# Feature projections in float32 on half the array, two items at a time, in a linear-attention and expert-MLP kernel

## The chip, the cores and the metric

The kernel runs on one core of a Trainium2 chip. The metric is the time of one execution on the device in microseconds (us). The engines are called as in the profile: PE (TensorE, with its weight loads as PEld), DVE (VectorE), ACT (ScalarE), POOL (GpSimd) and SP (SyncE, which issues most DMAs).

## The reference

Three layers in a row: linear attention with exponential features, a gated MLP, and a mixture of four experts. Only the first is touched by the change.

```python
batch, n_heads, seq, head_dim, d_feat = 2, 8, 576, 64, 128
def phi(x):
    proj = np.einsum('bhsd,df->bhsf', x, w_phi)
    proj = proj - np.max(np.abs(proj), axis=-1, keepdims=True)
    return np.concatenate([np.exp(proj), np.exp(-proj)], axis=-1)
q_p, k_p = phi(q), phi(k)
kv = np.einsum('bhsf,bhsd->bhfd', k_p, v)
z = np.sum(k_p, axis=2)
num = np.einsum('bhsf,bhfd->bhsd', q_p, kv)
den = np.einsum('bhsf,bhf->bhs', q_p, z)[..., None] + 1e-06
x = num / den                       # to [1152, 512]
x = ((x @ w_a) * (x @ w_b)) @ w_out # 1152 x 512, inner size 1536
out = sum over e of p[:, e] * (relu(x @ w1[e]) @ w2[e])   # 4 experts, inner size 1024
```

All inputs are float32.

## The kernel before

Heads are worked on in pairs: the 64 dimensions of one head lie on partitions 0 to 63, those of its partner on 64 to 127. A tile is 128 positions of a head pair. Since 576 is four tiles and a half, the half tiles of two head pairs share one tile, marked "m". An **item** is two tiles; there are 18 items for k and then 18 for q, nine for each of the two batches. Three items make a chunk of 768 columns of the transposed k or q, which SP loads as `xraw` (`load_chunk`).

One loop over slots writes the program of the attention (lines 765 to 803), and this hand-written order is the order of each engine's queue. Slot s issues, in this sequence:

- `split_x(s + 3)`: ACT rounds 256 columns of `xraw` to float32r (`xp`, high part) and POOL subtracts to get the low part, three slots ahead.
- `stage_proj(s)`: six float32r matmuls of 128 rows and 256 columns into one PSUM tile `pj`. The right side `wbp` is block diagonal: w_phi for head 0 in rows 0 to 63 and columns 0 to 127, for head 1 in the rest, zeros elsewhere. Three matmuls (high by high, high by low, low by high) make one tile. Then DVE takes the largest magnitude (`mx`) and subtracts it (`r`); for k, ACT makes the two exponentials (`kp`).
- `stage_kv(s - 3)` for k items: four float32 matmuls of 128 rows and 256 columns, or for an "m" tile four of 64 rows, which add to `kv`. A finished head pair is copied from PSUM by DVE (`kvt`), transposed on PE two slots later (`kz`) and copied again (`kvz`, by DVE in the first batch and by ACT in the second).
- `stage_rt(s - 4)` for q items: four PE transposes of `r` (`rt`), then ACT's exponentials (`qp`).
- What fell due: `stage_num` (eight float32 matmuls of 288 columns, `num`, read by ACT into `den` and `x`), one slot later `stage_x` on DVE (transpose of `den` to `dt`, reciprocal `rc`, spread back over `dt`, transpose to `rb`, product with `x`), then `stage_xparts` (`xh` on ACT, `xl` on POOL).
- Preparation of the weights of the MLP (`prep`: `begin` on ACT, `middle` on DVE, `parts` on ACT and POOL) in every second k slot and in the last slots, and in the last slots the first matmuls of the MLP (`unit_ab`).

The PSUM tiles of `pj`, `kz`, `rt` and `ab` share the pool `u` with four buffers; `kv` and `num` share `nd` with two. Behind the attention come `unit_ab`, `o1`, `unit_h` and `o2`, which make the two MLPs.

Of the kernel before, what the change touches and what calls it, by code (L numbers as in the profile page):

```python
# [9 lines left out]
F32 = mybir.dt.float32  # L10
F32R = mybir.dt.float32r
# [36 lines left out]
def tile_linear_attention_then_mlps(ctx, tc, qT, kT, v, w_phi, wab, wout, w12, probs, out):  # L48
# [19 lines left out]
    m_p = None  # L68
    l_p = None

    wb = r_p.tile([128, 2, 128], F32, tag="wb", name="wb")
    wbp = r_p.tile([128, 2, 256], F32R, tag="wbp", name="wbp")

    with tc.manual_schedule():
        nc.scalar.dma_start(out=wb[0:64, 0, :], in_=w_phi)
        nc.scalar.dma_start(out=wb[64:128, 1, :], in_=w_phi)
        nc.vector.memset(wb[0:64, 1, :], 0.0)
        nc.vector.memset(wb[64:128, 0, :], 0.0)

        nc.vector.memset(psm, 0.0)  # L80
        nc.scalar.activation(out=psm, in_=psm, func=AF.Exp)
# [1 line left out]
        def two_parts(hi, lo, src, eng):  # L83
            nc.scalar.activation(out=hi, in_=src, func=AF.Copy)  # L84
            eng.tensor_tensor(out=lo, in0=src, in1=hi.bitcast(F32), op=ALU.subtract)  # L85

        NC = 3 * 256
        xraw = {}
        xpart = {}

        def load_chunk(n):


            if n >= 2 * B * 3:
                return
            t = r_p.tile([128, NC], F32, tag="xraw", name="xraw", bufs=2)
            src = (kT if n < B * 3 else qT)[n % (B * 3)]
            step = 256 if n == 0 else NC
            for c in range(0, NC, step):
                nc.sync.dma_start(out=t[:, c:c + step], in_=src[:, c:c + step])  # L100
            xraw[n] = t

        def split_x(i, eng):
            n, c = i // 3, i % 3 * 256
            if c == 0:
                xpart[n] = [r_p.tile([128, NC], F32R, tag=f"xp{k}", name="xp", bufs=2) for k in range(2)]
            hi, lo = (t[:, c:c + 256] for t in xpart[n])
            if i == 0:
                nc.vector.tensor_copy(hi, xraw[n][:, 0:256])
                nc.vector.tensor_tensor(out=lo, in0=xraw[n][:, 0:256], in1=hi.bitcast(F32), op=ALU.subtract)  # L110
            else:
                two_parts(hi, lo, xraw[n][:, c:c + 256], eng)
            if c == 512:
                load_chunk(n + 2)
# [32 lines left out]
        for kind in "kq":  # L147
            for b in range(B):
                for g in range(9):
                    items.append((kind, b, g, seq[2 * g:2 * g + 2]))  # L150

        st_r = {}
        st_kp = {}
        kv_ps = {}
        kvt_t = {}
        kvz_t = {}
        qp_t = {}

        def stage_proj(i):
            kind, b, g, ts_ = items[i]  # L160
            ps = u_p.tile([128, 2, 2, 128], F32, tag="u", name="pj")
            for j in range(2):
                c = i % 3 * 256 + j * 128
                hi, lo = (t[:, c:c + 128] for t in xpart[i // 3])
                o = ps[:, j].rearrange("p h f -> p (h f)")
                nc.tensor.matmul(out=o, lhsT=hi, rhs=wbp[:, 0], start=True, stop=False)
                nc.tensor.matmul(out=o, lhsT=hi, rhs=wbp[:, 1], start=False, stop=False)
                nc.tensor.matmul(out=o, lhsT=lo, rhs=wbp[:, 0], start=False, stop=True)
            ps4 = ps.rearrange("p t h f -> p (t h) f")
            mx = r_p.tile([128, 4], F32, tag="mx", name="mx", bufs=4)  # L170
            nc.vector.tensor_reduce(out=mx, in_=ps4, op=ALU.max, axis=AX.X, apply_absolute_value=True)
            r = r_p.tile([128, 4, 128], F32, tag="r", name="r", bufs=6)
            nc.vector.tensor_tensor(
                out=r, in0=ps4, in1=mx.unsqueeze(2).to_broadcast([128, 4, 128]), op=ALU.subtract
            )
            st_r[i] = r
            if kind == "k":
                kp = k_p.tile([128, 4, 2, 128], F32, tag="kp", name="kp", bufs=4)
                nc.scalar.activation(out=kp[:, :, 0, :], in_=r, func=AF.Exp)
                nc.scalar.activation(out=kp[:, :, 1, :], in_=r, func=AF.Exp, scale=-1.0)  # L180
                st_kp[i] = kp

        def stage_kv(i):
            kind, b, g, ts_ = items[i]
            kp = st_kp[i]
            done = []
            for j, t in enumerate(ts_):
                if t[0] == "m":
                    parts = [(t[1], 4, 0, 64, False, True), (t[2], 4, 64, 128, True, False)]
                else:  # L190
                    first, last = t[1] == 0, t[1] == 3
                    parts = [(t[0], t[1], 0, 128, first and t[0] % 2 == 0, last and t[0] % 2 == 1)]
                for p, st, lo, hi, first, last in parts:
                    if first:
                        kv_ps[b, p] = nd_p.tile([128, 2, 512], F32, tag="nd", name="kv")
                    for h in range(2):
                        nc.tensor.matmul(
                            out=kv_ps[b, p][:, h, 0:256],
                            lhsT=vt[b][lo:hi, st, p, 64 * h:64 * h + 128],
                            rhs=kp[lo:hi, 2 * j + h].rearrange("p s f -> p (s f)"),  # L200
                            start=first, stop=last,
                        )
                    if last:
                        done.append((b, p))
            for b, p in done:
                t = k_p.tile([128, 2, 256], F32, tag="kvt", name="kvt", bufs=2)
                nc.vector.tensor_copy(t, kv_ps.pop((b, p))[:, :, 0:256])
                kvt_t[b, p] = t
            return done

# [2 lines left out]
        def stage_kvz(b, p):  # L213
            src = kvt_t.pop((b, p))
            ps = u_p.tile([128, 2, 2, 128], F32, tag="u", name="kz")
            for h in range(2):
                for s in range(2):
                    nc.tensor.transpose(out=ps[:, h, s, :], in_=src[:, h, 128 * s:128 * s + 128], identity=ident)
            t = kvz_all[:, b * NP + p].rearrange("p (h s f) -> p h s f", h=2, s=2)
            if b == B - 1:  # L220
                nc.scalar.activation(out=t, in_=ps, func=AF.Copy)
            else:
                nc.vector.tensor_copy(t, ps)
            kvz_t[b, p] = t

        def stage_rt(i):
            kind, b, g, ts_ = items[i]
            r = st_r[i]
            ps = u_p.tile([128, 2, 2, 128], F32, tag="u", name="rt")
            for j in range(2):  # L230
                for h in range(2):
                    nc.tensor.transpose(out=ps[:, h, j, :], in_=r[:, 2 * j + h, :], identity=ident)
# [55 lines left out]
            return x, den  # L288

        def stage_x(b, p, x, den):  # L290
            dt = q_p.tile([128, 18, 32], F32, tag="dt", name="dt", bufs=1)
            nc.vector.transpose(out=dt.rearrange("p a b -> p (a b)"), in_=den.rearrange("p a b -> p (a b)"))
            rc = q_p.tile([128, 18, 1], F32, tag="rc", name="rc", bufs=2)
            nc.vector.reciprocal(out=rc, in_=dt[:, :, 0:1])
            nc.vector.tensor_copy(dt, rc.to_broadcast([128, 18, 32]))
            rb = q_p.tile([128, 2, HT], F32, tag="rb", name="rb", bufs=1)
            nc.vector.transpose(out=rb.rearrange("p a b -> p (a b)"), in_=dt.rearrange("p a b -> p (a b)"))
            nc.vector.tensor_tensor(out=x, in0=x, in1=rb, op=ALU.mult)
# [408 lines left out]
        def run(gen, rate, tasks_per):  # L707
# [13 lines left out]


        load_chunk(0)
        load_chunk(1)
        alloc_v(0)
        load_v(0, 0)
        load_v(0, 1)
        make_identity(nc, ident)
        split_x(0, nc.vector)
        nc.vector.tensor_copy(wbp[:, 0], wb.rearrange("p h f -> p (h f)"))  # L730
        nc.vector.tensor_tensor(
            out=wbp[:, 1], in0=wb.rearrange("p h f -> p (h f)"), in1=wbp[:, 0].bitcast(F32), op=ALU.subtract
        )
        for i in range(1, 3):
            split_x(i, nc.vector)
        for st in range(2, 5):
            load_v(0, st)
        alloc_v(1)

        def probabilities():  # L740
# [24 lines left out]
        for slot in range(NI + 9):  # L765
            if slot < NI:
                kind, b, g, ts_ = items[slot]
                if slot + 3 < NI:
                    split_x(slot + 3, nc.gpsimd)
                stage_proj(slot)  # L770
            if slot == NK + 4:
                for fn, a in todo.pop(slot, []):
                    fn(*a)
# [109 lines left out]
```

## Time and profile before

| | us |
|---|---|
| median of 3 runs (lowest to highest) | 731.62 (731.14 to 731.96) |
| the profiled execution | 731.71 |
| its span, first to last instruction | 729.8 |
| PE busy | 716.4 (98%) |
| DVE busy | 431.0 (59%) |
| ACT busy | 325.8 (45%) |
| POOL busy | 304.0 (42%) |

The busy times hold for the whole span. The attention is the first seventh of it, and there the shares are others than on average, so the stages are to be read one by one. The profile models the end of a matmul; the distance of two starts tells more than the length of a row. An entry in brackets at a row's end is the idle time of the engine before it and what ended it.

### The profile page before, as it was taken

Reading aid. Unit: us, or ns where it says so; the run is one execution under the profiler, and the core shown is the slowest. Engines: PE = TensorE matmul, PEld = TensorE weight load, DVE = VectorE, ACT = ScalarE, POOL = GpSimd, SP = SyncE. Lnnn points to the kernel's source line nnn. Section 1 sums busy time; section 2 is a strip of 40 time slices with the busy share of each in tenths; the row PEclk is TensorE's granted clock in tenths of the full one; section 3 lists DMA queues with packets and bytes.
Section 4 is the critical chain, followed back from the end, with each engine's and each line's share of the span. In section 5 each row is a group of like instructions: output and inputs, shape, how many; then the busy total and the mean of one; then the engine's idle time right before and its main releaser. Section 6 shows DMA issues by size and latency. Waiting matters only on the chain.

```text
span 729.8 us, 11577 instructions
## 1 busy us (share of the span) xinstructions
PE 716.4 (98%) x4544; PEld 660.2 (90%) x4544; DVE 431.0 (59%) x737; ACT 325.8 (45%) x658; POOL 304.0 (42%) x277
## 2 busy tenths in 40 slices
PE   7999999999999999999899999999999999999998
PEld 6887879999999999999789898988988898989896
DVE  5997987566666664363635454545455545545454
ACT  5787996655444442233644232323233333423221
POOL 3664435554444343312783434434352535343300
PEclk9999999999999999999999999999999999999999
DMA  8643001332323231012031112110111111100003
GB/s 232 190 131 116 1 30 30 116 96 79 115 64 106 64 87 30 11 49 87 3 114 30 43 46 58 30 58 30 58 55 33 31 58 58 30 30 0 1 1 129
DMA packets 37798, 46.18 MB, mean 63 GB/s; under 512 B 5616, under 2 KB 26608, under 8 KB 37744
## 3 DMA queue, kind: packets, MB, share of 16 engines
q1 hardware_dynamic: 37440, 45.25, 20.7%
q8 instruction: 35, 0.57, 0.3%
q10 hardware_dynamic: 304, 0.20, 0.1%
q14 instruction: 19, 0.16, 0.1%
HBM read 43.08 MB, written 2.36 MB: 62 GB/s over the span
## 4 chain that ended last, share of the span: by engine, by line
PE 85%; DVE 8%; ACT 3%; DMA 2%; issue 1%; POOL 0%; DVEq 0%; SPq 0%; POOLq 0%
PE acc L680 9%; PE acc L679 9%; PE acc L678 9%; PE ab L608 6%; PE ab L606 6%; PE ab L607 6%; PE X L531 5%; PE X L532 5%; PE X L533 5%; PE acc L637 3%; PE acc L638 3%; PE acc L636 3%; PE num L275 3%; PE Z L532 2%; PE Z L531 2%; PE Z L533 2%
## 5 line engine op out<-in xcount | busy, mean ns | idle before, releaser
L694 DVE SCALAR_TENSOR_TENSOR oacc<-acc,pr,oacc 128x512 f32<-128x512 f32 (+1 forms) x136 | 101.3, 746 | 117.5 <-PE acc L680 117.5
L85 POOL TENSOR_TENSOR w<-wx,w 128x512 fp32r<-128x512 f32 x68 | 91.5, 1346 | 155.2 <-ACT w L84 155.2
L85 POOL TENSOR_TENSOR wc<-wt,wc 128x512 fp32r<-128x512 f32 (+1 forms) x48 | 70.0, 1490 | 109.6 <-ACT wc L84 109.6
L680 PE MATMUL acc<-w,hhb 128*128 128x512 f32 x288 | 114.0, 396 | 0.9 <-DVE hhb L655 0.9
L606 PE MATMUL ab<-xh,w 128*128 128x288 f32 x384 | 113.5, 296 | 0.0
L608 PE MATMUL ab<-xh,w 128*128 128x288 f32 x384 | 113.1, 295 | 0.0
L679 PE MATMUL acc<-w,hhb 128*128 128x512 f32 x288 | 113.1, 393 | 0.0
L607 PE MATMUL ab<-xl,w 128*128 128x288 f32 x384 | 113.0, 294 | 0.0
L678 PE MATMUL acc<-w,hhb 128*128 128x512 f32 x288 | 112.7, 391 | 0.0
L654 ACT ACTIVATE hhb<-h 128x288 fp32r<-128x288 f32 x64 | 36.2, 565 | 96.2 <-DVE h L539 96.1
L531 PE MATMUL X<-xc,wc 128*128 128x288 f32 x256 | 77.2, 301 | 1.4 <-ACT h L536 1.4
L532 PE MATMUL X<-xc,wc 128*128 128x288 f32 x256 | 75.8, 296 | 0.7 <-DVE xc L85 0.7
L533 PE MATMUL X<-xc,wc 128*128 128x288 f32 x256 | 75.4, 295 | 0.0
L536 ACT ACTIVATE h<-X 128x288 f32<-128x288 f32 x64 | 26.0, 407 | 104.7 <-PE X L533 104.7
L607 PEld LDWEIGHTS ab<-xl,w 128*128 128x128 f32 x384 | 72.0, 188 | 0.1
L606 PEld LDWEIGHTS ab<-xh,w 128*128 128x128 f32 x384 | 72.0, 188 | 0.1
L608 PEld LDWEIGHTS ab<-xh,w 128*128 128x128 f32 x384 | 72.0, 188 | 0.0
L680 PEld LDWEIGHTS acc<-w,hhb 128*128 128x128 f32 x288 | 54.0, 188 | 15.7 <-DVE hhb L655 4.4
L376 POOL TENSOR_TENSOR wx<-wx,rn 128x512 uint32<-128x512 uint32 x36 | 47.0, 1306 | 50.8 <-DVE wx L373 50.8
L655 DVE SCALAR_TENSOR_TENSOR hhb<-h,hhb 128x288 fp32r<-128x288 f32 x64 | 40.5, 633 | 42.2 <-ACT hhb L654 42.2
L679 PEld LDWEIGHTS acc<-w,hhb 128*128 128x128 f32 x288 | 54.0, 188 | 8.4
L678 PEld LDWEIGHTS acc<-w,hhb 128*128 128x128 f32 x288 | 54.1, 188 | 7.7
(104 smaller groups left out, 1655.0 us busy)
## 6 DMA issues: line engine op xcount, KB each, us to landing
raw<-in_wab SPq DMA_DIRECT2D x24, 512.0 KB, 3.8
wt<-in_w SPq DMA_DIRECT2D x64, 128.0 KB, 2.4
wx<-in_w SPq DMA_DIRECT2D x32, 256.0 KB, 3.0
raw<-in_wout SPq DMA_DIRECT2D x12, 512.0 KB, 3.7
xraw<-in_qT SPq DMA_DIRECT2D x6, 384.0 KB, 3.1
out<-oacc SPq DMA_DIRECT2D x8, 256.0 KB, 2.0
xraw<-in_kT SPq DMA_DIRECT2D x5, 384.0 KB, 3.6
v<-in_v SPq DMA_DIRECT2D x8, 192.0 KB, 4.4
```

The source lines that it names most:

```text
L85: eng.tensor_tensor(out=lo, in0=src, in1=hi.bitcast(F32), op=ALU.subtract)
L376: nc.gpsimd.tensor_tensor(out=x, in0=x, in1=r, op=ALU.add)
L531: nc.tensor.matmul(out=ps, lhsT=whi, rhs=xhi, start=first and a == 0, stop=False, skip_group_check=True)
L532: nc.tensor.matmul(out=ps, lhsT=whi, rhs=xlo, start=False, stop=False, skip_group_check=True)
L533: nc.tensor.matmul(out=ps, lhsT=wlo, rhs=xhi, start=False, stop=a == 1, skip_group_check=True)
L606: nc.tensor.matmul(out=t, lhsT=whi, rhs=hi, start=(c == 0), stop=False)
L607: nc.tensor.matmul(out=t, lhsT=whi, rhs=lo, start=False, stop=False)
L608: nc.tensor.matmul(out=t, lhsT=wlo, rhs=hi, start=False, stop=(c == KD - 1))
L678: nc.tensor.matmul(out=acc, lhsT=hi, rhs=w[:, 0, f], start=f == 0, stop=False)
L679: nc.tensor.matmul(out=acc, lhsT=hi, rhs=w[:, 1, f], start=False, stop=False)
L680: nc.tensor.matmul(out=acc, lhsT=lo, rhs=w[:, 0, f], start=False, stop=f == 1)
L694: nc.vector.scalar_tensor_tensor(out=oc, in0=acc[:, c:c + step], scalar=sc, in1=oc, op0=ALU.mult, op1=ALU.add)
```

## The change

- The projections of two items are issued together, in every even slot, as eight float32 matmuls of 64 rows and 128 columns straight from `xraw`: four with the lower 64 partitions (head 0) into one PSUM tile, then four with the upper 64 (head 1) into another. `wb` holds w_phi twice, on the lower and on the upper partitions. The splits into `xp` and `wbp` are gone.
- `mx`, `r` and `kp` of two items are now made one tile for each head; `feat` finds the piece that `kv` and `rt` need. `r` has eight buffers, `kp` six, `xraw` three.
- The copies `kvt`, `kvz` and the spreading of the reciprocals over `dt` are all done by ACT (`copy`); `dt` has two buffers.
- At the start the first rows of v are issued before the second chunk, and a third chunk is loaded ahead.

```diff
-    wb = r_p.tile([128, 2, 128], F32, tag="wb", name="wb")
-    wbp = r_p.tile([128, 2, 256], F32R, tag="wbp", name="wbp")
+    wb = r_p.tile([128, 128], F32, tag="wb", name="wb")
...
-        nc.scalar.dma_start(out=wb[0:64, 0, :], in_=w_phi)
-        nc.scalar.dma_start(out=wb[64:128, 1, :], in_=w_phi)
-        nc.vector.memset(wb[0:64, 1, :], 0.0)
-        nc.vector.memset(wb[64:128, 0, :], 0.0)
+        nc.scalar.dma_start(out=wb[0:64], in_=w_phi)
+        nc.scalar.dma_start(out=wb[64:128], in_=w_phi)
...
-            t = r_p.tile([128, NC], F32, tag="xraw", name="xraw", bufs=2)
+            t = r_p.tile([128, NC], F32, tag="xraw", name="xraw", bufs=3)
...
-        def split_x(i, eng):
...
+        def feat(st, i, j, h):
+            return st[i // 2][h][:, 2 * (i % 2) + j]
...
         def stage_proj(i):
-            kind, b, g, ts_ = items[i]
-            ps = u_p.tile([128, 2, 2, 128], F32, tag="u", name="pj")
-            for j in range(2):
-                c = i % 3 * 256 + j * 128
-                hi, lo = (t[:, c:c + 128] for t in xpart[i // 3])
-                o = ps[:, j].rearrange("p h f -> p (h f)")
-                nc.tensor.matmul(out=o, lhsT=hi, rhs=wbp[:, 0], start=True, stop=False)
-                nc.tensor.matmul(out=o, lhsT=hi, rhs=wbp[:, 1], start=False, stop=False)
-                nc.tensor.matmul(out=o, lhsT=lo, rhs=wbp[:, 0], start=False, stop=True)
...
+            for h in range(2):
+                ps = u_p.tile([128, 4, 128], F32, tag="u", name="pj")
+                for n in (i, i + 1):
+                    for j in range(2):
+                        c = n % 3 * 256 + j * 128
+                        nc.tensor.matmul(
+                            out=ps[:, 2 * (n - i) + j], lhsT=xraw[n // 3][64 * h:64 * h + 64, c:c + 128],
+                            rhs=wb[64 * h:64 * h + 64], start=True, stop=True,
+                        )
+                pss.append(ps)
+            for n in (i, i + 1):
+                if n % 3 == 2:
+                    load_chunk(n // 3 + 3)
+            st_r[i // 2], st_kp[i // 2] = [], []
+            for ps in pss:
+                mx = r_p.tile([128, 4], F32, tag="mx", name="mx", bufs=4)
+                nc.vector.tensor_reduce(out=mx, in_=ps, op=ALU.max, axis=AX.X, apply_absolute_value=True)
+                r = r_p.tile([128, 4, 128], F32, tag="r", name="r", bufs=8)
...
-                nc.vector.tensor_copy(t, kv_ps.pop((b, p))[:, :, 0:256])
+                copy(t, kv_ps.pop((b, p))[:, :, 0:256])
...
-            if b == B - 1:
-                nc.scalar.activation(out=t, in_=ps, func=AF.Copy)
-            else:
-                nc.vector.tensor_copy(t, ps)
+            copy(t, ps)
...
-            dt = q_p.tile([128, 18, 32], F32, tag="dt", name="dt", bufs=1)
+            dt = q_p.tile([128, 18, 32], F32, tag="dt", name="dt", bufs=2)
...
-            nc.vector.tensor_copy(dt, rc.to_broadcast([128, 18, 32]))
+            copy(dt, rc.to_broadcast([128, 18, 32]))
...
         load_chunk(0)
-        load_chunk(1)
         alloc_v(0)
         load_v(0, 0)
+        load_chunk(1)
         load_v(0, 1)
...
-                if slot + 3 < NI:
-                    split_x(slot + 3, nc.gpsimd)
-                stage_proj(slot)
+                if slot % 2 == 0:
+                    stage_proj(slot)
```

On PE, slot 8 begins after the last kv matmuls of slot 7 and a transpose group `kz`. Before, it reads (three of the six matmuls of item 8 are shown):

```order
L197 MATMUL kv_270<-kp_226,v_102 128x256 x2
L197 MATMUL kv_335<-kp_226,v_102 128x256 x2
L218 MATMUL kz_340<-ident_61,kvt_275 128x128 x4
L166 MATMUL pj_352<-wbp_86,xp_190 128x256
L167 MATMUL pj_352<-wbp_86,xp_190 128x256
L168 MATMUL pj_352<-wbp_86,xp_191 128x256
```

The same place of the changed kernel, where `pj_297` is the lower half and `pj_302` the upper, and each reads two chunks because items 8 and 9 lie in different ones:

```order
L213 MATMUL kz_289<-ident_61,kvt_234 128x128 x4
L156 MATMUL pj_297<-wb_85,xraw_117 128x128 x2
L156 MATMUL pj_297<-wb_85,xraw_155 128x128 x2
L156 MATMUL pj_302<-wb_85,xraw_117 128x128 x2
L156 MATMUL pj_302<-wb_85,xraw_155 128x128 x2
L192 MATMUL kv_284<-kp_196,v_97 128x256
L192 MATMUL kv_284<-kp_203,v_97 128x256
```

Two items' projections now stand in one row, all of the lower half before all of the upper, and kv reads two `kp` tiles, one for each head.

On DVE, the first division of the q items (`stage_x` of the first `num`) stands before the next `mx`. Before:

```order
L173 TENSOR_TENSOR r<-pj,mx 128x512
L292 STREAM_TRANSPOSE dt<-den 128x576
L294 RECIPROCAL rc<-dt 128x18
L295 COPY dt<-rc 128x576
L297 STREAM_TRANSPOSE rb<-dt 128x576
L298 TENSOR_TENSOR x<-x,rb 128x576
L171 TENSOR_REDUCE mx<-pj 128x4
```

And in the changed kernel:

```order
L169 TENSOR_TENSOR r<-pj,mx 128x512
L283 STREAM_TRANSPOSE dt<-den 128x576
L285 RECIPROCAL rc<-dt 128x18
L288 STREAM_TRANSPOSE rb<-dt 128x576
L289 TENSOR_TENSOR x<-x,rb 128x576
L167 TENSOR_REDUCE mx<-pj 128x4
```

The copy between `rc` and `rb` has left DVE for ACT's queue, so `rb` waits for ACT.

## Rows read from the trace of the kernel before

**Rows 1.** Stages: bounds, length, busy PE, PEld, DVE, ACT, POOL, granted clock, DMA.

```profile
4.50:62.00 57.50, 56.75 (x334) 49.88 (x334) 49.47 (x85) 42.00 (x86) 32.71 (x36) 1.00 0.64 185
62.00:94.50 32.50, 31.73 (x196) 27.31 (x195) 27.41 (x44) 29.66 (x70) 12.32 (x14) 1.00 0.09 28
94.50:108.60 14.10, 13.59 (x65) 10.65 (x64) 12.14 (x19) 12.62 (x28) 4.34 (x4) 1.00 0.11 35
...
128.60:729.80 601.20, 594.36 (x3818) 553.26 (x3816) 325.92 (x565) 226.06 (x451) 240.03 (x210) 1.00 0.18 55
```

**Rows 2.** Timeline of PE in k items: start, length, what.

```profile
12.53 0.28 PE L166 MATMUL pj<-wbp,xp 128*128 128x256 f32 x1
...
12.88 1.89 PE L197 MATMUL kv<-kp,v 128*128 128x256 f32 x8
...
14.97 0.28 PE L166 MATMUL pj<-wbp,xp 128*128 128x256 f32 x1
...
15.41 2.20 PE L197 MATMUL kv<-kp,v 64*128 64x256 f32 x12
...
17.81 0.28 PE L166 MATMUL pj<-wbp,xp 128*128 128x256 f32 x1
```

**Rows 3.** Chain of waits, one period of q items: start, length, what.

```profile
80.47 3.88 PE num L275 x16
...
85.06 0.44 PE rt L232 x4
...
86.66 3.90 PE num L275 x16
```

**Rows 4.** PE's waits from 0 to 130 us: total, times, longest.

```profile
PE pj L166 <- DVE wbp L730: 4.6, 1, 4.6
PE pj L166 <- DVE r L173: 0.9, 2, 0.5
PE num L275 <- ACT x L287: 0.5, 1, 0.5
```

**Rows 5.** Timeline of DVE, one period of q items.

```profile
80.25 0.77 DVE L292 STREAM_TRANSPOSE dt<-den 128x576 f32<-128x576 f32 x1
...
81.36 0.67 DVE L295 COPY dt<-rc 128x576 f32<-128x576 f32 x1
82.07 0.78 DVE L297 STREAM_TRANSPOSE rb<-dt 128x576 f32<-128x576 f32 x1
...
83.85 0.68 DVE L171 TENSOR_REDUCE mx<-pj 128x4 f32<-128x512 f32 x1
84.56 0.69 DVE L173 TENSOR_TENSOR r<-pj,mx 128x512 f32<-128x512 f32 x1
...
86.49 0.77 DVE L292 STREAM_TRANSPOSE dt<-den 128x576 f32<-128x576 f32 x1
```

**Rows 6.** Timeline of PE's weight loads in k items.

```profile
12.77 1.60 PEld L197 LDWEIGHTS kv<-kp,v 128*128 128x128 f32 x8
...
15.41 0.74 PEld L197 LDWEIGHTS kv<-kp,v 64*128 64x128 f32 x8
```

**Rows 7.** Groups by line, ACT, 0 to 140 us: busy us, mean ns, idle before.

```profile
L84 ACT ACTIVATE xp<-xraw 128x256 fp32r<-128x256 f32 x35 | 14.2, 411 | 1.5 <-DMA xraw<-in_kT 1.4
L179 ACT ACTIVATE kp<-r 128x512 f32<-128x512 f32 x18 | 11.3, 626 | 11.0 <-DVE r L173 10.0 <-PE kv L197 0.5 <-PE pj L168 0.4
...
L303 ACT ACTIVATE xh<-x 128x576 fp32r<-128x576 f32 x8 | 5.5, 683 | 1.4 <-DVE x L298 1.2
```

**Rows 8.** Timeline of PE at the start.

```profile
4.56 0.58 PE L166 MATMUL pj<-wbp,xp 128*128 128x256 f32 x1 [4.56 <-DVE wbp L730]
...
9.88 0.41 PE L168 MATMUL pj<-wbp,xp 128*128 128x256 f32 x1
10.09 2.24 PE L197 MATMUL kv<-kp,v 128*128 128x256 f32 x8
```

**Rows 9.** Timeline of ACT at the start.

```profile
4.45 0.42 ACT L84 ACTIVATE xp<-xraw 128x256 fp32r<-128x256 f32 x1 [0.64 <-DMA xraw<-in_kT]
```

More of the change, by code (lines that the diff above doesn't have):

```diff
@@ L88, in tile_linear_attention_then_mlps @@
         xraw = {}
-        xpart = {}
         def load_chunk(n):
@@ L101, in load_chunk @@
             xraw[n] = t
-        def split_x(i, eng):
[L104 to L110, printed above, removed]
-            else:
-                two_parts(hi, lo, xraw[n][:, c:c + 256], eng)
-            if c == 512:
-                load_chunk(n + 2)
         vt = {}
@@ L169, in stage_proj @@
[L169 to L181, printed above, removed]
+            kind = items[i][0]
@@ new lines, in stage_proj @@
+            pss = []
+            for h in range(2):
[8 more added lines that the diff above has]
+                pss.append(ps)
@@ new lines, in stage_proj @@
+            for n in (i, i + 1):
[6 more added lines that the diff above has]
+                r = r_p.tile([128, 4, 128], F32, tag="r", name="r", bufs=8)
+                nc.vector.tensor_tensor(
+                    out=r, in0=ps, in1=mx.unsqueeze(2).to_broadcast([128, 4, 128]), op=ALU.subtract
+                )
+                st_r[i // 2].append(r)
+                if kind == "k":
+                    kp = k_p.tile([128, 4, 2, 128], F32, tag="kp", name="kp", bufs=6)
+                    nc.scalar.activation(out=kp[:, :, 0, :], in_=r, func=AF.Exp)
+                    nc.scalar.activation(out=kp[:, :, 1, :], in_=r, func=AF.Exp, scale=-1.0)
+                    st_kp[i // 2].append(kp)
@@ L183, in stage_kv @@
         def stage_kv(i):
             kind, b, g, ts_ = items[i]
-            kp = st_kp[i]
             done = []
@@ L199, in stage_kv @@
                             lhsT=vt[b][lo:hi, st, p, 64 * h:64 * h + 128],
-                            rhs=kp[lo:hi, 2 * j + h].rearrange("p s f -> p (s f)"),
+                            rhs=feat(st_kp, i, j, h)[lo:hi].rearrange("p s f -> p (s f)"),
                             start=first, stop=last,
@@ L219, in stage_kvz @@
             t = kvz_all[:, b * NP + p].rearrange("p (h s f) -> p h s f", h=2, s=2)
-            if b == B - 1:
-                nc.scalar.activation(out=t, in_=ps, func=AF.Copy)
-            else:
-                nc.vector.tensor_copy(t, ps)
+            copy(t, ps)
             kvz_t[b, p] = t
@@ L227, in stage_rt @@
             kind, b, g, ts_ = items[i]
-            r = st_r[i]
             ps = u_p.tile([128, 2, 2, 128], F32, tag="u", name="rt")
@@ L231, in stage_rt @@
                 for h in range(2):
-                    nc.tensor.transpose(out=ps[:, h, j, :], in_=r[:, 2 * j + h, :], identity=ident)
+                    nc.tensor.transpose(out=ps[:, h, j, :], in_=feat(st_r, i, j, h), identity=ident)
             for t in ts_:
@@ L723, in tile_linear_attention_then_mlps @@
         load_chunk(0)
-        load_chunk(1)
         alloc_v(0)
         load_v(0, 0)
+        load_chunk(1)
         load_v(0, 1)
         make_identity(nc, ident)
[L729 to L735, printed above, removed]
         for st in range(2, 5):
             load_v(0, st)
+        load_chunk(2)
         alloc_v(1)
```

## The prediction

> **What bounds the kernel now.** I read the table of stages first, then TensorE's timeline in each stage, then the engines beside it. The table [rows 1] cuts the span at 62 us, where the k items end, at 94.5, where the last projection of a q item is over, and at 108.6, where the first expert matmuls fill in. PE is busy 56.75 of the first 57.5 us, 31.73 of the next 32.5, 13.59 of 14.1, and 594.36 of the last 601.2. A busy PE need not be a full one, so I looked at starts: in the k items one item, six projections and four kv matmuls, lasts 12.53 to 14.97, 2.44 us [rows 2]. Three projections take 12.53 to 12.88, 0.117 to 0.119 each, 0.71 for six; that leaves 1.73 us for the 8 records of kv, 0.216 each, and two passes of 256 columns at 2.4 GHz are 0.213. No gap is left: PE is full there. In the q items one period (two projections 1.43, two rt 0.88, eight num 3.88) makes 6.19 us, which is also the distance of two num groups [rows 3]. PE's waits in the first 130 us come to some 7 us, 4.6 of them the first [rows 4]. So what counts is PE's work and new PE waits in the first 130 us; the 600 us behind are the same instructions, and move as a block.
>
> Second to PE stands DVE. In the q items it runs almost without a gap with a period of 6.24 us (80.25 to 86.49) [rows 5], as long as PE's; ACT is busy 29.66 of 32.5 us [rows 1]. A saving on PE alone can be lost there.
>
> **The change part by part.**
>
> *The projection itself.* Before, two items cost 12 matmuls x 0.119 = 1.43 us. After, it is eight float32 matmuls of 64 rows and 128 columns. A float32 matmul shows as two records: kv, 256 columns, has 8 records for 4 matmuls [rows 2], so a matmul is four passes of its columns. At 128 columns the passes of one record are 0.108 us; its weight load is no shorter, since rt, 128 columns and one pass, takes 0.44 us for 4, 0.11 each [rows 3]. So a record costs 0.11 to 0.12 us, and the 16 records of a pair of items 1.76 to 1.9 us in series. Whether the halves (partitions 0 to 63 and 64 to 127) run side by side decides. The trace has a case: the item that starts at 15.41 with four 64-row kv matmuls, two of the lower half and then two of the upper [rows 2]. Their eight loads take 0.74 us, where eight loads of 128 rows take 1.60 [rows 6], and the item lasts 14.97 to 17.81, 2.84 us. With halves side by side its array work equals a normal item's, 2.44; one after the other it would be 0.86 more, 3.30. So they do overlap, though issued in the order lower, lower, upper, upper, and the 0.40 left over is the price of going into 64-row work and back. I take 8 x 0.11 + 0.40 = 1.28 us a pair, bounds 1.22 (0.108 a record, 0.36 for the change of mode) and 1.35 (0.12): -0.15 us, from -0.21 to -0.08, against 1.43. This is an estimate: the trace has two matmuls a half, the change four.
>
> The Trainium skill's page "TensorE: Matmul & The Clock Gate", section "The mechanism" in Part 3, speaks against the change: MATMULs start and end strictly in program order. By that rule only the last record of the lower half would overlap the first of the upper. By that rule the sum would be some 10 us higher. The 0.74 us of [rows 6] disagree with it for two matmuls a half; the first rival below is what is left of it for four.
>
> *k items.* Of 18 pairs, two fall in the opening (below), 7 in the rest of the k items: 7 x -0.15 = -1.05. One pair stands directly before a half tile of kv (items 14 and 15) and saves one change of mode, -0.4. DVE loses twelve 128x512 copies, and PE's two waits for r, 0.9 us [rows 4], may shrink: -0.4, bounds 0 and -0.9. The copies go to ACT, where xp's 0.41 us each [rows 7] end; ACT was busy 42.0 of 57.5 us [rows 1]. New is the batching: kp of an item must be there when its kv comes. Between a pair's projections and its first kv, PE has three kv items and the next projections, 3 x 1.73 + 1.28 = 6.5 us. The path is two maxima and two r on DVE, 2 x 1.35 [rows 5], then two exponentials of 0.63 [rows 7]: 4.0. That leaves 2.5 us for DVE's weight preparation queued ahead, so I put no wait there. Sum -1.9, bounds -2.8 and -0.6.
>
> *q items.* PE could save 9 x 0.15 = 1.35 us. But DVE keeps its chain: dt, rc, then a copy that is now ACT's, rb, x, and four projection instructions. The copy was 0.71 us of DVE's time (81.36 to 82.07) [rows 5]; on ACT the nearest row is xh, of the same size, 0.68 [rows 7], and DVE must wait for it at rb, with everything queued behind (x and the maxima that free the PSUM tiles of the next projections). So DVE's period stays about 6.2, and PE's saving turns into waiting. I take 0; bounds -1.35 (the x product has less of GpSimd's traffic beside it and DVE falls under PE's period) and +1.5 (0.3 us of waiting at rb in each of five periods).
>
> *After the last projection.* ACT is busy 12.62 of 14.1 us there [rows 1] and PE already waits 0.5 us for its x [rows 4]. xp is no longer there to be removed; two dt copies of 0.6 to 0.68 come in ahead of the next den and x. PE's wait grows by one of them, with a little more at the end: +0.8, bounds 0 and +2.
>
> *The opening.* Before, PE starts at 4.56 after DVE has split x and w_phi [rows 8], and runs four items' projections at 0.21 us a matmul (9.88 to 10.09 [rows 8]); kv follows at 10.09. After, no split is waited for, but a pair needs the second third of the chunk, which landed by 4.45 [rows 9]. The upper half then takes 8 x 0.21 = 1.7, to 6.3; DVE's two maxima and two r 2.7; the exponentials 0.6 each behind them: the first kv can start fully at 9.5. So PE stands from about 8 to 9.5. The clock matters here: 256 columns in 0.21 us is the 1.2 GHz level, 0.117 at 12.53 is the 2.4 GHz level [rows 2, 8] (the granted-clock column of [rows 1] reads 1.00 throughout), and the change came while PE worked without a gap. If it comes as early as before, the opening gains 0.6 us and most of what the first kv lost: -0.8. If PE's new gap delays it by about 5 us of work, that work takes twice its time: +2.5. I take +0.8, nearer the middle.
>
> GpSimd loses 33 subtractions; PE waits for none of them now. SP's v rows move ahead of the second chunk; the bytes are the same, and the second chunk is needed only by the second pair.
>
> **Sum**, on the profiled execution's own 731.7 (span 729.8): +0.8 - 1.9 + 0 + 0.8 = -0.3, so 731.4. The median of the runs is 731.6, 0.1 lower, so 731.3. All lower bounds together: -0.8 - 2.8 - 1.35 + 0 = -5.0, 726.7; all upper ones: +2.5 - 0.6 + 1.5 + 2 = +5.4, 737.
>
> **Rivals.** (1) *Halves in series.* The upper half's four matmuls stand 16 instructions behind the lower's first, against 8 in the kv case; if the queue doesn't reach that far, a pair costs 15 x 0.11 + 0.40 = 2.05, +0.62 on 16 pairs, +9.9: about 741.5. The rule of the Trainium skill's page "TensorE: Matmul & The Clock Gate" on program order would do the same. For it: no row has so deep a queue. Against: [rows 6]. A middle form, the upper half starting four records late, is 12 x 0.11 + 0.40 = 1.72, +4.6: 736. (2) *Slower by the hop at rb.* ACT reaches dt late, since qp and den stand ahead of it; DVE then frees the pair's two PSUM tiles late, and the next pair needs both at once. From 0.4 us a period on, five periods and the end cost over 3 us: 734.5. For it: three engines with nearly the same period [rows 1, 3, 5]. Against: rc itself comes late on a full DVE, so ACT may be there first. (3) *Faster:* the clock rises as before, PE's saving in the q items is real and the end costs nothing: near 727.5. For it: DVE and GpSimd lose work in every stage. That the change shortens nothing on PE (a record of 0.12, mode change 0.40 or more) is inside the forecast's own bounds.
>
> **How the numbers follow.** 0.2% is 1.5 us, about what a measurement of this kernel can tell from no change. Forecast, small terms that cancel: 0.33. Rival 3: 0.28. Rival 2: 0.17. Series 0.14, middle form 0.08. So faster 0.28, same 0.33, slower 0.39. The range runs from 727.3 to 737.0 (all upper bounds, and the middle form); outside are the series case and a few hundredths below. The likeliest case's own range is 730 to 733.
>
> **What would show it.** Right: eight projections of a pair in about 0.9 us with lower and upper starts a few hundredths apart; k periods of two items near 4.9 - 0.15; PE waits for r or x under 2 us after the opening; the 600 us behind unchanged. Wrong: a pair near 1.7 to 1.9 us (rival 1); DVE idle before rb, released by ACT, with PE idle before pj released by r (rival 2); the change of pace from 0.21 a record before 9 us or after 13 us (the opening's two ends).

## The result and the profile after

The changed kernel takes 741.54 us (median of 4 runs, 741.21 to 741.74), the kernel before 731.38 beside it (730.84 to 731.96): a ratio of 1.0138, 95% interval 1.0121 to 1.0156, 10 us slower. Predicted were 731.3 us and a range up to 737.0. The profiled execution has a span of 739.4 us, 9.6 more than before.

Where they go is read from the starts of four PE operations in both traces: the projections of the fifth item, the first `rt`, the first expert matmul (`ab`) and the first `acc`.

| stretch | before | after | difference | predicted |
|---|---|---|---|---|
| to the fifth item's projections (opening) | 11.98 | 14.04 | +2.06 | +0.8 |
| on to the first `rt` (k items) | 49.63 | 52.20 | +2.57 | -1.9 |
| on to the first `ab` (q items and what follows them) | 47.02 | 49.06 | +2.04 | +0.8 with the next |
| on to the first `acc` | 19.97 | 20.65 | +0.68 | |
| behind it, some 360 us into the span | | | +2.0 | 0 |

The third mark does not part quite the same work: before, the first `rt` has the projections of 23 items ahead of it, in the changed kernel those of 24 (12 whole pairs). An item's projections cost 0.71 us before, so like for like the k items stand at about +1.9 and the stretch behind them at about +2.7.

The last row is a fall of the clock that some executions of nearly every kernel here have, the kernel before included. All four of the changed kernel had it (mean clock 0.998). Of the four of the kernel before beside them only the profiled one has its clock on record (1.000); the others' times, up to 731.96, lie below those of its executions on record that lost the clock (732.52 and more).

**A pair's projections.** PE's timeline of the changed kernel in the k items (start, length, what; x counts records, two for a float32 matmul):

```profile
33.19 3.72 PE L192 MATMUL kv<-kp,v 128*128 128x256 f32 x16
36.74 0.60 PE L213 MATMUL kz<-ident,kvt 128*128 128x128 f32 x4
37.27 1.71 PE L156 MATMUL pj<-wb,xraw 64*128 64x128 f32 x16
38.91 3.72 PE L192 MATMUL kv<-kp,v 128*128 128x256 f32 x16
42.47 0.60 PE L213 MATMUL kz<-ident,kvt 128*128 128x128 f32 x4
```

From 37.27 to 38.91 a pair holds PE for 1.64 us. Before, kv, kz and the projections of two items came round in 5.32 us (19.70 to 25.02); now it is 5.73 (37.27 to 43.00): +0.41 a pair. With all that belongs to it a pair so costs 1.43 + 0.41 = 1.84 us, where 1.28 was predicted. The same 1.64 us in thirds, the instructions of `pj` alone (bounds, length, busy PE with its matmul records, PEld with its loads, DVE, clock, DMA):

```profile
37.26:37.81 0.55, 0.54 (x4) 0.54 (x5) 0.00 (x0) 1.00 0.00 0
37.81:38.36 0.55, 0.55 (x10) 0.55 (x9) 0.00 (x0) 1.00 0.70 82
38.36:38.91 0.55, 0.55 (x7) 0.43 (x4) 0.44 (x1) 1.00 0.39 141
```

Five loads fall in the first third, nine in the second, four in the last (one that reaches over a bound is counted on both sides): the halves overlap only in the middle. In the single records of the pair at 43.00 the upper half's first load starts at 43.554, with the lower's sixth (43.553); the other pairs of the k items have the same 0.554 us between the halves. After that both advance by 0.11 us a record.

**The opening.** PE's timeline:

```profile
3.13 3.63 PE L156 MATMUL pj<-wb,xraw 64*128 64x128 f32 x20 [3.13 <-DMA wb<-in_w_phi]
8.56 2.09 PE L156 MATMUL pj<-wb,xraw 64*128 64x128 f32 x12 [1.80 <-DMA xraw<-in_kT]
10.58 3.53 PE L192 MATMUL kv<-kp,v 128*128 128x256 f32 x8
14.04 1.71 PE L156 MATMUL pj<-wb,xraw 64*128 64x128 f32 x16
```

The second pair waits 1.80 us for the second chunk. Eight kv records then take 3.46 us (10.58 to 14.04), 0.43 each, which is the 1.2 GHz level; before, the same eight took 1.89, since the pace rose after 10.09 [rows 8].

**PE's waits in the first 140 us** (total, times, longest), which answer to [rows 4]:

```profile
PE pj L156 <- DMA xraw<-in_kT: 1.8, 1, 1.8
PE num L266 <- ACT x L278: 1.1, 1, 1.1
PE rt L223 <- ACT qp L241: 0.8, 1, 0.8
PE acc L628 <- DVE hhb L610: 0.4, 1, 0.4
```

The waits for `r` are gone. The wait for `x` has doubled, from 0.5 to 1.1.

**Far behind.** The windows of the second part of the span (columns as in [rows 1]):

```profile
136.00:365.00 229.00, 227.08 (x1687) 224.99 (x1686) 133.23 (x243) 100.10 (x185) 94.29 (x79) 1.00 0.23 72
365.00:369.00 4.00, 3.38 (x15) 3.38 (x16) 1.45 (x2) 2.85 (x7) 2.63 (x2) 0.57 0.02 4
369.00:739.40 370.40, 365.66 (x2117) 326.29 (x2116) 191.67 (x321) 123.68 (x261) 143.10 (x130) 1.00 0.14 44
```

Between 365 and 369 the granted clock is 0.57 on average; matmuls of 288 columns stand 0.24 us apart there instead of 0.13. It follows directly on a wait of PE that both kernels have:

```profile
365.62 0.61 PE L522 MATMUL X<-xc,wc 128*128 128x288 f32 x1 [1.40 <-ACT h L527]
```

### The profile page after: what moved, and what is told of

Same layout as the page of the kernel before. It is cut to its first block, busy times and chain, and to the rows that moved or that the text cites. A ratio compares the mean times of both kernels' runs of the same rounds, so it can differ in the third digit from the quotient of the medians.

```text
span 739.4 us, 11629 instructions
## 1 busy us (share of the span) xinstructions
PE 724.9 (98%) x4616; PEld 663.3 (90%) x4616; DVE 415.4 (56%) x709; ACT 326.0 (44%) x643; POOL 278.2 (38%) x244
## 4 chain that ended last, share of the span: by engine, by line
PE 92%; DVE 3%; ACT 2%; issue 1%; DMA 1%; SPq 0%; POOL 0%; DVEq 0%; ACTq 0%; POOLq 0%
PE acc L671 9%; PE acc L670 9%; PE acc L669 9%; PE ab L599 6%; PE ab L597 6%; PE ab L598 6%; PE kv L192 5%; PE X L522 5%; PE X L523 4%; PE X L524 4%; PE pj L156 4%; PE acc L628 3%; PE acc L629 3%; PE acc L627 3%; PE num L266 3%; PE Z L522 2%
```

## The experiments

Three theories stood for the 0.554 us between the halves: PE looks only a few instructions ahead in its queue for work of the other half; the upper half's PSUM tile comes free late; the queue issues instructions at a fixed pace. The first four kernels part these, and the projections from the copies.

**Lower, upper, lower, upper.**

```diff
-            pss = []
-            for h in range(2):
-                ps = u_p.tile([128, 4, 128], F32, tag="u", name="pj")
-                for n in (i, i + 1):
-                    for j in range(2):
...
+            pss = [u_p.tile([128, 4, 128], F32, tag="u", name="pj") for _ in range(2)]
+            for h, n, j in [(h, n, j) for n in (i, i + 1) for j in range(2) for h in range(2)]:
```

> The eight projections of a pair are issued lower, upper, lower, upper, instead of four lower and then four upper; nothing else. In the changed kernel the upper half starts 0.554 us after the lower in every pair, right after the lower's fifth record. Theory 1 (PE looks only some four records ahead in its queue for work of the other half): the halves now run side by side from the start, a pair falls from about 1.8 to 1.28 us, 16 pairs x 0.55 = -8.8: about 732.7. Theory 2 (the upper half's PSUM tile comes free 0.55 us later, so its first matmul waits for DVE): the start of the upper half stays late, now with the lower half blocked behind it, about 741 or more. Theory 3 (the queue issues an instruction each 0.035 us, and 16 stand between): upper half 0.07 us late, nearly as theory 1, about 733.5.

Measured: 733.29 us, ratio 1.0008 (0.9992 to 1.0024), where the changed kernel had 1.0138: by the ratios 9.5 us of its 10 are gone. Part of that is the clock: executions with a mean clock of 0.997 or 0.998 have spans of 732.4 to 732.9 here and of 739.4 to 740.0 in the changed kernel, 7 us apart. PE's timeline, then one pair in halves as above:

```profile
34.63 1.16 PE L153 MATMUL pj<-wb,xraw 64*128 64x128 f32 x16
35.72 3.72 PE L188 MATMUL kv<-kp,v 128*128 128x256 f32 x16
39.28 0.60 PE L209 MATMUL kz<-ident,kvt 128*128 128x128 f32 x4
39.81 1.16 PE L153 MATMUL pj<-wb,xraw 64*128 64x128 f32 x16
```

```profile
34.62:35.17 0.55, 0.54 (x8) 0.54 (x10) 0.00 (x0) 1.00 0.27 106
35.17:35.72 0.55, 0.55 (x12) 0.43 (x8) 0.00 (x0) 1.00 0.09 34
```

Ten loads fall in the first 0.55 us instead of five, the pair takes 1.09 us instead of 1.64, and kv, kz and a pair come round in 5.18 us (34.63 to 39.81). Before it was 5.32: that is the -0.14 us a pair which the prediction put at -0.15. The theory of the late PSUM tile falls for the k items: same tiles, same releases, no late half. In the q items three pairs (at 61.85, 64.83 and 83.40 us) do start their upper half 0.4 to 0.6 us late.

**Two and two.** The same edit with the order `for n in (i, i + 1) for h in range(2) for j in range(2)`.

> The same eight projections issued two lower, two upper, two lower, two upper, which is the order of the 64-row kv matmuls that ran side by side. Theory 1 (a look-ahead of some four records): two matmuls are four records, so the upper half starts at once, 733. Theory 2 (PSUM tile late): as the changed kernel, 741. Theory 3 (0.035 us an instruction): eight instructions stand between, upper half 0.28 us late, about 737.

Measured: 733.24 us, ratio 1.0017 (1.0008 to 1.0027).

```profile
35.15 1.26 PE L153 MATMUL pj<-wb,xraw 64*128 64x128 f32 x16
36.34 3.72 PE L188 MATMUL kv<-kp,v 128*128 128x256 f32 x16
```

A pair takes 1.19 us. In the single records of the pair at 45.27 the upper half starts 0.013 us after the lower, though eight instructions stand between them; the theory of a fixed pace of issue (0.28 us) falls too. The Trainium skill's page "TensorE: Matmul & The Clock Gate", section "The mechanism" in Part 3, has matmuls start and end in program order; here the upper half's first matmul started at 45.289 and the lower's second, which stands ahead of it, at 45.600. So the measurement decides against that rule for matmuls of different halves.

**Three, three, one, one.** The order `for ms in ((0, 1, 2), (3,)) for h in range(2) for m in ms`, with m counting the four matmuls of a half.

> The changed kernel with the eight projections issued three lower, three upper, one lower, one upper. It measures the depth of the look-ahead. With four and four the upper half starts together with the lower's sixth weight load, three records (three loads and three matmuls) before the lower half's last one is through; with two and two at once. If PE looks a fixed number of instructions ahead, the upper half starts here together with the lower's fourth load, 0.33 us after the lower's first, and a pair takes about 1.09 + 0.33 = 1.4 us; about 736 to 738. If the depth is not a number of instructions, the start is at 0.01 or at 0.55 us.

Measured: 736.57 us (one run).

```profile
36.50 1.49 PE L153 MATMUL pj<-wb,xraw 64*128 64x128 f32 x16
37.92 3.72 PE L188 MATMUL kv<-kp,v 128*128 128x256 f32 x16
```

A pair takes 1.42 us, 0.33 more than alternating. In the single records of the pair at 47.08 the upper half's first load starts at 47.405, with the lower's fourth at 47.404. So with two, three and four matmuls ahead the upper half starts with the lower's first, fourth and sixth load, that is 0.01, 0.33 and 0.55 us late. In all three, six instructions of the lower half that stand ahead of it (three loads, three matmuls) had still to begin just then: a look-ahead over a fixed number of instructions, not a time. Whether the limit counts instructions, loads or matmuls these runs do not part, since each load has one matmul.

**The copies, all back on DVE, and all on ACT alone.** The changed kernel with DVE's copies:

```diff
-                copy(t, kv_ps.pop((b, p))[:, :, 0:256])
+                nc.vector.tensor_copy(t, kv_ps.pop((b, p))[:, :, 0:256])
...
-            copy(dt, rc.to_broadcast([128, 18, 32]))
+            nc.vector.tensor_copy(dt, rc.to_broadcast([128, 18, 32]))
```

> The changed kernel with its copies of kvt, kvz and the reciprocals (dt) back on DVE; projections and order as changed. If the copies on ACT cost at the end of the attention stage (PE waits there 0.8 us for qp and 1.1 us for x, where the kernel before waited 0.5 us): 1 to 2 us faster than the changed kernel, about 740. If the copies relieve DVE in the q items, as the change has it, it gets slower: with PE's period now 6.55 us and DVE's 6.2 there is room on DVE, so at most 1 us, 742.5.

Measured: 738.16 us, ratio 1.0072 (1.0044 to 1.0099), 4.8 us less than the changed kernel by the ratios, much of it the clock, which two of its four executions kept. The two that lost it (0.998) have spans of 737.3 and 737.5, 2.3 us below the changed kernel's at the same clock, little more than the 1 to 2 of the forecast. And the kernel before with `copy` in all three places and two buffers for `dt`:

> The kernel before with nothing but its copies of kvt, kvz (all) and dt moved to ACT, dt with two buffers; projections as before. By the prediction's terms: DVE must wait for ACT at rb in each of five periods of the q items (0 to +1.5) and PE waits longer for x after the last projection (0 to +2); the k items gain at most 0.4. Forecast +0.8 us: 732.2. If it comes out at +0.3 or less, the copies are free and all of the loss lies in the projections; at over +2, the hop at rb is a cause of its own.

Measured: 735.30 us, ratio 1.0045 (1.003 to 1.006): 3.3 us slower by the copies alone (the one execution that kept its clock has a span of 733.0, those of the kernel before that did 729.1 to 730.9), so the copies are a cause of their own. Next they were taken apart.

**The copy of dt alone.** Only the last line of that edit, in the kernel before (two buffers):

> The kernel before with only the copy of dt moved to ACT (two buffers). It prices the prediction's second rival, the hop at rb, by itself. From the pairs so far (all copies on ACT: +1.6 us at the end of the attention stage; in the alternating kernel dt's return to DVE gains 1.6 with the opening apart, more): the whole loss of the copies is here, +1.5 to +2.5 us, ratio 1.002 to 1.0035. If the hop is hidden as the prediction has it: ratio 1.000 to 1.001.

Measured: 735.72 us, ratio 1.0046 (1.003 to 1.0063): all of it is here. DVE's timeline in one period of its q items, then ACT's:

```profile
79.59 0.77 DVE L292 STREAM_TRANSPOSE dt<-den 128x576 f32<-128x576 f32 x1
80.40 0.27 DVE L294 RECIPROCAL rc<-dt 128x18 f32<-128x18 f32 x1
82.11 0.78 DVE L297 STREAM_TRANSPOSE rb<-dt 128x576 f32<-128x576 f32 x1 [1.45 <-ACT dt L536]
```

```profile
80.42 1.09 ACT L250 ACTIVATE qp<-rt 128x512 f32<-128x512 f32 x2
81.39 0.69 ACT L536 ACTIVATE dt<-rc 128x576 f32<-128x576 f32 x1
```

`rc` is done at 80.67, but ACT begins the copy at 81.39, behind `qp`, and `rb` starts at 82.11: 1.45 us of idle DVE. Before, DVE made the same copy in 0.67 us [rows 5]. DVE's period becomes 6.78 (the next `dt` starts at 86.37), while the distance of two `num` on PE stays 6.18: DVE falls behind in each period, and PE pays when it runs out of projections. From the fourth `num` (85.83) to the fifth (95.30) it is 9.47 us here, and 8.02 before (86.49 to 94.51). PE's waits from 62 to 130 us show where it pays; before, the same three were 0.4, 0.5 and 0.2:

```profile
PE pj L166 <- DVE r L173: 1.1, 2, 0.8
PE num L275 <- ACT x L287: 1.1, 1, 1.1
PE rt L232 <- ACT qp L250: 0.6, 1, 0.6
```

**The copies of kvt and kvz alone.** The other two lines of the edit, in the kernel before:

> The kernel before with only the copies of kvt and of the first batch's kvz moved to ACT. In the alternating kernel, kvt and kvz on ACT rather than on DVE are worth about 1 us (undisturbed spans near 727 against 728.7). If they relieve DVE, ratio 0.9985 to 0.9995. If PE waits for kvt on a full ACT (1.2 us at a kv, with all copies on ACT): ratio 1.0015.

Measured: 731.51 us, ratio 0.9996 (0.9982 to 1.001): no difference.

**dt's copy in the changed kernel.** Only `dt` back on DVE, the order of the projections as changed:

> The changed kernel, order of the projections as changed, with only the copy of dt back on DVE. If the hop at rb costs although PE's period in the q items is longer now (6.55 us): the first expert matmul comes 1.5 to 2.5 us earlier than in the changed kernel, 739 to 740 with the clock's drop. If PE's longer period hides it up to the last projection, only the end's wait for x is left: 0.5 to 1 us, 740.7.

Measured: 736.35 us, ratio 1.0060 (1.0047 to 1.0074). The four executions had no fall of the clock. The first `ab` stands at 113.02 (115.30 in the changed kernel), the first `acc` at 133.00 (135.95). Part of the first is an opening that came 0.85 us earlier (13.19 against 14.04); the two stretches from the first `rt` on are 1.42 and 0.67 us shorter, 2.1 together. Up to the last projections nothing is gained: the distance of two `num` is 6.54 to 6.55 in both. PE's waits from 62 to 130 us:

```profile
PE rt L223 <- ACT qp L241: 0.8, 1, 0.8
```

The waits for `x` (1.1) and `xl` (0.3) are gone. So in the changed kernel the hop costs behind the last projection, not in the periods.

**Alternating, with both kinds of copies on DVE.**

> The changed kernel with its projections issued lower, upper, lower, upper, and the copies of kvt, kvz and dt back on DVE: what is left of the change is the projection alone, in float32 on raw inputs by pairs. If the two losses add (order: the first expert matmul 7.5 us late with fours and 0.6 with alternation, so 6.9; copies: 7.5 against 5.8, so 1.7), it stands at 0.6 - 1.7 = -1.1 us against the kernel before: ratio 0.9985. If they overlap (DVE, given its copies back, becomes the bound of the q items when PE is faster), it gains less than 1 us on the alternating kernel: ratio 1.000 or more.

Measured: ratio 1.0017 (1.0002 to 1.0032). In the profiled execution, which kept its clock, the first `ab` stands 1.12 us before that of the kernel before and the span is 728.7: so far the sum of the two losses is as expected. But 9 of 12 executions had a mean clock of 0.998 or less, and their spans were 730.7 to 733.9; the ratio does not show the gain. PE's waits up to 145 us name what else is lost:

```profile
PE pj L153 <- DVE r L165: 1.8, 2, 1.3
```

**Alternating, with only dt's copy on DVE.**

> The alternating kernel with only the copy of dt back on DVE; kvt and kvz stay on ACT. It tells which copies cost the 1.7 us. If the hop of dt (PE waits 1.1 us for x, where the kernel before waited 0.5): most of the gain of DVE's copies is here, ratio 0.9990. If kvt (in the kernel before with ACT's copies, PE waits 1.2 us at a kv for it): no gain over the alternating kernel, ratio 1.0005.

Measured: 729.08 us, ratio 0.9953 (0.9935 to 0.9972), the fastest kernel of the study and faster than both kernels of the case; I had expected 0.9990 at best. Much of the distance to the kernel with all copies on DVE is the clock, which five of six executions kept here and three of twelve there. Among those that kept it the spans are 726.1 to 727.6 here, 728.7 to 729.7 there, and 729.1 to 730.8 in the kernel before. The same wait is here:

```profile
PE pj L153 <- DVE r L165: 0.4, 1, 0.4
```

On a DVE that also copies `kvt` and `kvz`, PE waits 1.4 us more for `r`; with faster projections those copies are worth moving, with slow ones they are not (above, 0.9996). From the fifth item's projections to the first `rt` it is 47.91 us here and 49.18 with DVE's copies (46.93 and 46.82 in two later kernels with the same attention part); two `num` are 6.00 us apart (74.17 to 80.17), where the kernel before has 6.19 [rows 3].

**The second chunk first, in thirds.** The kernel with all copies on DVE, with

```diff
-            step = 256 if n == 0 else NC
+            step = 256 if n < 2 else NC
...
-        load_v(0, 0)
         load_chunk(1)
+        load_v(0, 0)
```

> The kernel of the alternating order with DVE's copies, and besides it the second chunk of k is loaded ahead of the first rows of v and in three parts, so that the second pair of projections waits for one part alone. The theory of the opening (PE stands for the second chunk, 0.5 us in the alternating kernel and 1.8 in the changed one, and reaches its full clock later): the projections of the fifth item start at 12.0 instead of 12.8 us, -0.8: ratio 0.9975. Rival: the rows of v come later by the chunk's 0.38 MB and the first kv waits for them instead, ratio 0.9985 to 1.000.

Measured: ratio 1.0016 (1.0002 to 1.0029), the same as without it. PE's timeline at the start:

```profile
4.22 3.30 PE L153 MATMUL pj<-wb,xraw 64*128 64x128 f32 x30 [0.26 <-DMA wb<-in_w_phi]
8.62 0.67 PE L188 MATMUL kv<-kp,v 128*128 128x256 f32 x2 [1.09 <-ACT kp L172]
9.90 2.58 PE L188 MATMUL kv<-kp,v 128*128 128x256 f32 x6 [0.61 <-ACT kp L172]
12.40 1.77 PE L153 MATMUL pj<-wb,xraw 64*128 64x128 f32 x16
```

The wait for the chunk is gone, and waits for `kp` have come in its place, 1.7 us together; the fifth item starts at 12.40 (12.33 without the edit). Neither theory named that wait: it is the chain from `pj` over DVE and ACT to the first kv. What the edit is worth stays open, because none of its twelve executions kept the clock (0.993 to 0.998), and in the profiled one it fell twice in the attention, where the kernel without the edit shows 1.00 (columns as in [rows 1]):

```profile
10.30:13.70 3.40, 3.40 (x18) 2.48 (x18) 0.97 (x2) 2.02 (x4) 0.00 (x0) 0.50 0.67 188
58.00:62.00 4.00, 4.00 (x16) 3.10 (x16) 3.67 (x6) 0.17 (x1) 0.00 (x0) 0.57 0.40 117
```

So part of the 12.40 is the clock. The second fall stands behind a wait of 1.34 us for `r` (ended at 56.62), which the kernel without the edit has too (ended at 55.94) and passed without a fall in its profile.

**The fall of the clock.** Ten matmuls, whose result the next product overwrites, ahead of the product that waits at 365 us:

```diff
+            for _ in range(10 if (u, tp) == (("1", 0), 0) else 0):
+                nc.tensor.matmul(out=Z, lhsT=w[:, 0, M2[0], 0:128], rhs=x[:, 0, M2[1], 0, :], start=True, stop=True)
             product(X, w, x, M6, False)
```

> The changed kernel with ten matmuls more, whose result is overwritten, in the place where PE waits 1.40 us in the first unit of the second expert layer (some 360 us into the span). There, in the changed kernel, the granted clock fell to half for 3.4 us and cost 2.0 us; the kernel before has the same wait and kept its clock in the execution shown. If the idle time lets the clock fall: clock 1.000 and 739.5 us. If something else does, or the drop is only moved: 0.998 and 741.5 us or more.

Measured: 740.77 us, clock 1.000 in all four executions. But the edit sits in the wrong unit, with the ten at 328.38, some 38 us before the wait ends (366.6), which is still there (1.39 us). So the idle time alone does not make the clock fall. The same in the kernel with the best ratio:

> The alternating kernel with dt's copy on DVE and those of kvt and kvz on ACT (729.1 us, ratio 0.9953), with the same ten matmuls in the same place. If the idle time there is what lets the clock fall, every execution keeps it: about 728.8, and the executions lie closer together. If not, 729.1 to 729.5.

Measured: ratio 0.9977 (0.9967 to 0.9987); 2 of 12 executions at 0.997. With `tp` 1 in the condition the ten matmuls stand in the wait itself:

> The changed kernel with ten matmuls more in the unit in which PE waits 1.40 us for ACT, directly ahead of the matmul that waits; their result is overwritten. If the idle time is what the drop of the clock needs: clock 1.000 in all executions, the wait at most 0.2 us, 739.5 us. If the drop comes as often with the wait filled (it hangs on something else that the executions do not share): 0.998 in some or all, 741.5 us.

Measured: 739.22 us, ratio 1.0098 (1.0082 to 1.0115); clock 1.000 in all four. PE's timeline there, and the window of seven microseconds around the place, here and then in the changed kernel:

```profile
364.79 1.49 PE L546 MATMUL Z<-xc,wc 128*128 128x288 f32 x10
366.35 0.40 PE L522 MATMUL X<-xc,wc 128*128 128x288 f32 x1
```

```profile
362.00:369.00 7.00, 6.23 (x43) 5.60 (x43) 2.79 (x3) 5.79 (x11) 4.04 (x4) 1.00 0.01 2
```

```profile
362.00:369.00 7.00, 4.90 (x24) 4.48 (x24) 2.56 (x3) 4.65 (x9) 4.12 (x3) 0.76 0.01 2
```

> The alternating kernel with dt's copy on DVE, with the same ten matmuls in the same place. If the idle time lets the clock fall: no execution at a clock of 0.997 (1 of 6 had it), spans 726 to 728, median about 728.8. If not: 729.1 to 730.

Measured: 729.23 us, ratio 0.9962 (0.9948 to 0.9977), no execution of six below 0.999. Against the kernel without the ten matmuls (0.9953) that is no measurable difference. With the wait filled, none of ten executions lost the clock; with the wait left, some do and some do not, and with the ten matmuls 38 us ahead of it none of four did in the changed kernel. So the runs do not show that it is the filled wait which keeps the clock. What decides it is open: the kernel before has the same wait and lost its clock in 6 of the 24 executions that ran beside the second group of kernels.

## Why the prediction was wrong

**The step that failed** is the price of a pair. The half tile of kv showed two matmuls of each half side by side [rows 2, 6], and I carried that to four ("So they do overlap, though issued in the order lower, lower, upper, upper"). The estimate was marked as such, but the forecast stood on it and only two rivals, 0.22 together, on its failing. Four matmuls stand beyond PE's look-ahead; the pair cost 5.73 - 5.32 = +0.41 instead of -0.15. By alternation alone it became -0.14. So the sizes in that step (0.11 a record, 0.40 for the mode) were right and its premise was wrong. What happened is the middle form of the first rival, five records late rather than four. It had the chance of 0.08. That the series rival's 741.5 us is the measured time is an accident: in series a pair was to cost +0.62, and here +0.41 a pair, the copies, the opening and the clock make up the same sum.

**k items**: -1.9 predicted, +2.57 measured, about +1.9 like for like. With alternating halves the same stretch is -2.04 (47.59 against 49.63), about -2.7 like for like. The terms that do not hang on the order were sound: PE's waits for `r`, 0.9 us [rows 4], did go, 0.5 of it in this stretch.

**q items**: 0 predicted, because DVE's period of 6.24 [rows 5] would hold PE. In the changed kernel PE's period is 6.55 against 6.19, +0.36 for the same slow pair; PE itself sets it, so DVE's relief bought nothing. With alternating halves and `dt` on DVE it is 6.00: the saving on PE (0.19) was real, and the reading of DVE as a wall was too strict.

**After the last projection**: +0.8 predicted, 0 to +2. The copy of `dt` alone cost 2.1 us there in the changed kernel, and 2.9 in the kernel before (49.18 + 20.68 us against 47.02 + 19.97). The mechanism is the second rival's, ACT late at `dt` behind `qp`, but not at its place: in the changed kernel DVE's waits of 1.3 to 2.0 us in the periods with projections cost PE nothing, and those behind them cost everything. In the kernel before half of the 2.9 comes at the last projections (9.47 against 8.02 us), where PE waits for `r` and `qp`. The term was right in sign and too small by 1.3 us or more.

**The opening**: +0.8 predicted, -0.8 to +2.5; +2.06 measured. The pace rose late, as the upper bound had it, but PE's gap was another: the prediction let PE stand for the first `kp` and put no wait on the second chunk, and PE stood 1.80 us for that chunk and not for `kp`. In the kernels with the same loads in the opening the fifth item starts at 13.2 to 14.4 us with four and four, and at 12.3 to 13.7 alternating, so much of this term belongs to an execution and not to the kernel.

**Behind 130 us**: "move as a block" held for the order (all 3952 matmul records from the first `ab` on are the same) and failed by 2.0 us for the clock. I had no term for it. It is not the change's own work: the kernel before has such falls too, and two kernels with ten matmuls more, in the wait (739.2) or 38 us ahead of it (740.8), had none in four executions each.

The sum by what was measured: 2.06 + 2.57 + 2.04 + 0.68 + 2.0 = 9.35 of 9.6 us; the rest is spread behind 369 us.

## What to carry to other kernels

Let matmuls that are to run side by side on the two halves of the array alternate in program order, or stand in short runs: here two and two overlapped and lost 0.10 us a group against alternation, three and three lost 0.33 us and four and four 0.55 us a group. A case that overlaps in the trace says how far the queue has to reach in that case; count the instructions between the partners before carrying it to a longer run. And before a copy moves to another engine, look at what stands ahead of it in that engine's queue when its input is ready. The same copy was 0.67 us in place and 1.45 us of waiting elsewhere, while another copy moved to the same engine was worth more than a microsecond once the stage had become fast enough to need it.

## What the runs showed of the hardware

- PE's work on the lower and the upper 64 rows runs out of program order, but only over a short stretch of the queue: the upper half's first load began when six instructions of the lower half (three loads, three matmuls) had still to begin, and not sooner, whether four, six or eight pairs of a load and a matmul stood ahead.
- Eight pairs of a load and a matmul on each half, 64 rows and 128 columns in float32, take 0.9 us side by side at full clock, 0.11 a record, and some 0.2 us pass between the start of the last of them and that of the first load of 128 rows (46.266 to 46.466 in the two-and-two kernel).
- A wait of PE of 1.40 us, behind one of 0.69 and in a stretch that is otherwise full, was followed in some executions by a granted clock of 0.57 over the next four microseconds, which cost 2 us; in others the same wait passed without it, and with the wait filled by ten matmuls it was not seen in ten executions, nor in four with the ten matmuls 38 us ahead of the wait. What decides it is not shown.
